# Cluster masks of an attention kernel computed in strips of 32 rows instead of 64, for two units at once

## The chip, the cores and the metric

The kernel runs on one core of one Trainium2 chip. The metric is the device time of one execution in microseconds (us). Times inside the execution come from one profiled run, whose span from the first to the last instruction was 786.4 us; TensorE was granted 0.997 of its full clock.

## The reference

The program is an attention block in which a query sees only the keys of its own cluster, followed by a router over eight experts. Cut to what matters here:

```python
# q, k, v: (B=4, H=8, S=768, D=64); centroids: (8, 16, 64)
q_assign = argmax(q_n @ c_n.T)          # cluster of each query, 16 clusters a head
k_assign = argmax(k_n @ c_n.T)          # cluster of each key
mask = q_assign[..., :, None] == k_assign[..., None, :]
scores = 0.125 * q @ k.T
attn = softmax(where(mask, scores, -1e9))
x = (attn @ v)                          # then (B,H,S,D) -> (3072, 512)
# router: each row of x goes to one of 8 experts:
# out[rows of e] = gate * relu(x[rows] @ w1[e]) @ w2[e]
```

## The kernel before

**Two stages.** Attention takes roughly the first 360 us and the experts the rest; only attention is touched. The 32 pairs of batch and head are taken two heads at a time, which gives 16 head pairs. Each head pair has 2 halves of 384 queries and 6 blocks of 128 keys, 12 units, 192 in all. A unit is the scores of 128 keys by 384 queries for both heads. Its accumulator `s_ps` is 2 banks of PSUM (the accumulator memory that TensorE writes), one for each head, and the pool has two such buffers, so two units fill all four banks.

**The mask as a product.** The mask isn't applied by a selection. Every token has a code of three numbers (the columns 0, 1, 2 of `cd`), made so that the product of the codes of a key and a query is minus a huge number times the squared difference of the two cluster numbers: zero in the same cluster and hugely negative in any other. That product is added in the accumulator to the scores, and exp makes of it zero. `cd` holds a token's code in 64 columns for each of two heads, of which three are used; turned so that codes stand on partitions, head 0 takes rows 0 to 63 and head 1 rows 64 to 127. `choose` (L342, L345) writes the code columns from the cluster numbers `pm` on ScalarE, a transposing DMA turns them into `hot`, and `keys` (L375) copies the keys' half into `kH` on GpSimd. For the first head pair TensorE turns them (L362).

**A unit on TensorE.** `scores` (L437) issues for one unit four products: the two masks (`s_ps<-hot,kH`, bf16) and the two scores (`s_ps<-qT,kT`, f32), all with 64 rows of contraction. The two heads use the two halves of the rows of the array, so that they run side by side. `expo` (L448) is ScalarE's exp of the finished unit into `prob` (five buffers). `attend` (L457) multiplies `prob` with the values: 128 rows of contraction, 64 columns a head, both heads side by side in the columns. VectorE adds the `prob` tiles up in `acc` (L466, L476) for the denominators, and `total` (L491) sums those over partitions on TensorE in four column strips of 32.

**The order of the work** is written out by hand for all five engines. The main loop takes two units an iteration, 96 iterations. An iteration issues, in this order: for each of the two units two places ahead, `scores` and then `expo`; a piece of other work (`between`: cluster products L319 of the next head pair, codes, routing of an earlier batch); and `attend` of the two current units. At every third iteration `total` follows. So TensorE runs in one iteration: masks and scores of unit m, masks and scores of unit m+1, then the values' products of units m-2 and m-1. Unit m's masks write the buffer that unit m-2's exp has read, and unit m+1's masks that of unit m-1. The last iteration has no scores left to issue, so there are 95 such groups; units 0 and 1 come in `begin`.

Of the kernel before, what the change touches and what calls it, by code (L numbers as in the profile page):

```python
# [9 lines left out]
F32 = mybir.dt.float32  # L10
BF16 = mybir.dt.bfloat16
# [7 lines left out]
P = 128  # L19

SQ = 32
# [18 lines left out]
def kernel(  # L40
# [121 lines left out]
    tau = smp.tile([E, 1], F32, name="tau", bufs=1)  # L162


    cd = const.tile([P, S // (2 * SQ), 2, D], BF16, name="cd")
    wcd = const.tile([P, 1], F32, name="wcd")
    cn_r = smp.tile([P, 1], F32, name="cn_r", bufs=1)
    cn2 = smp.tile([P, 2, D], F32, name="cn2", bufs=1)
# [22 lines left out]
    def constants():  # L191
        nc.vector.memset(onesb, 1.0)
        keep_up(9)
        nc.vector.memset(epsc, EPS)
        make_identity(nc, ident)
        nc.gpsimd.iota(io_i, pattern=[[1, P]], base=0, channel_multiplier=0)

        nc.gpsimd.iota(
            tok_i.rearrange("p (b j) -> p b j", j=NJ),
            pattern=[[S, B], [P, NJ]],  # L200
            base=0,
            channel_multiplier=1,
        )
        for i, (p0, w) in enumerate(((0, -BIG), (D, -2.0))):
            nc.gpsimd.memset(wcd[p0 : p0 + D], w)
        make_identity(nc, identb)
        nc.gpsimd.memset(cd, 0.0)
        for i, (p0, c) in enumerate(((0, -BIG), (D, -1.0))):
            nc.gpsimd.memset(cd[p0 : p0 + D, :, :, 2 - 2 * i : 3 - 2 * i], c)
        make_upper_triangular(nc, sltb, val=1.0, diag=False)  # L210
        nc.gpsimd.memset(tri, 0.0)
        for e in range(1, E):
            nc.gpsimd.memset(tri[:, e, 0:e], 1.0)
        nc.vector.memset(cnB, 0.0)
        nc.vector.memset(ones, 1.0)
        nc.vector.memset(embT, 0.0)
        nc.vector.memset(cumx[:, 0], 0.0)
        nc.vector.memset(eb[:, 0:2], 0.0)
        nc.vector.tensor_copy(io_b, io_i)
        nc.vector.tensor_copy(io_f, io_i[0:1, 0:NBLK])  # L220
        nc.vector.tensor_scalar(prefc, io_b[:, 0:C], -1.0, float(C), ALU.mult, ALU.add)
        nc.vector.tensor_scalar(prefe, io_b[:, 0:E], -1.0, float(E), ALU.mult, ALU.add)
# [34 lines left out]
    def begin():  # L257

        nc.scalar.dma_start(out=c_sb, in_=centroids.rearrange("h c d -> (h c) d"))
        load(0, "q")  # L260
        load(0, "k")
        load(0, "v")
        load(1, "qk")
        constants()

        nc.scalar.activation(en_r, epsc[0:E], ACTF.Sqrt)
        nc.scalar.dma_start(out=emb, in_=moe_expert_emb)
        nc.scalar.dma_start(out=tau, in_=moe_tau.to_broadcast([E, 1]))
        norm_rows(cn_r, c_sb, P)
        unit_centroids()  # L270
        keep_up(2)
        piece(0, "turn0")
        piece(0, "turn1")
        norm_rows(en_r, emb, E)

        nc.scalar.activation(cn_r, epsc, ACTF.Exp)
        piece(0, "products")
        for m in range(2):
            scores(m, (1,))
        piece(0, "choose")  # L280
        keep_up(6)
        piece(0, "turn_numbers")
        for m in range(2):
            scores(m, (0,))
            expo(m)
        piece(0, "values")
        token_numbers()
        unit_experts()

    def prep_pieces(n):  # L290
# [39 lines left out]
        def choose():  # L330

            shp = [P, S // SQ, C]
            asn = t["asn"].rearrange("p (g c) -> p g c", c=C)
            amax = smp.tile(shp[0:2], F32, tag="amax", name="amax")
            sel = smp.tile(shp, BF16, tag="sel", name="sel", bufs=1)
            pm = smp.tile(shp[0:2], BF16, tag="pm", name="pm")
            nc.vector.tensor_reduce(amax, asn, axis=AXX, op=ALU.max)
            nc.vector.tensor_tensor(sel, asn, bc(amax, shp, 2), ALU.is_equal)
            nc.vector.tensor_tensor(sel, sel, bc(prefc, shp, 1), ALU.mult)
            nc.vector.tensor_reduce(pm, sel, axis=AXX, op=ALU.max)  # L340
            pm = pm.rearrange("p (s h) -> p s h", h=2)
            nc.scalar.activation(cd[..., 1], pm, ACTF.Copy, scale=wcd)  # L342
            for i, p0 in enumerate((0, D)):
                g = slice(p0, p0 + D)
                nc.scalar.activation(  # L345
                    cd[g, :, :, 2 * i], pm[g], ACTF.Square, scale=(BIG**0.5, 1.0)[i]
                )
            t["H"] = trp.tile([P, S // (2 * SQ), P], BF16, tag="hot", name="hot")
            if n > 0:
                nc.sync.dma_start_transpose(  # L350
                    out=t["H"], in_=cd.rearrange("p s h c -> p (s h c)")
                )

        def turn_numbers():

            t["kH"] = trp.tile([P, S], BF16, tag="kH", name="kH")
            kH = t["kH"].rearrange("r (i s t) -> r s i t", i=2, t=SQ)
            U = S // (4 * SQ)
            for half in range(2):
                bk = misc().bitcast(BF16)  # L360
                for u in range(U):
                    nc.tensor.transpose(  # L362
                        bk[:, P * u : P * u + P],
                        cd[:, U * half + u].rearrange("p h c -> p (h c)"),
                        identb,
                    )
                bk = bk[:, 0 : P * U].rearrange("r (s x) -> r s x", x=P)
                ss = slice(U * half, U * half + U)
                nc.scalar.copy(kH[:, ss], bk[:, :, D:].rearrange("r s (i t) -> r s i t", t=SQ))
                nc.vector.tensor_copy(t["H"][:, ss, 0:D], bk[:, :, 0:D])  # L370
# [49 lines left out]
    gr = [dict() for _ in range(ngroups)]  # L420
    xT = {}

    def scores(i, parts=(0, 1)):

        n, hq, j = units[i]
        t = ld[n]
        if "s_ps" not in un[i]:
            un[i]["s_ps"] = psS.tile([P, 2, 512], F32, tag="s_ps", name="s_ps")
        s_ps = un[i]["s_ps"]
        for part in parts:  # L430
            if part == 0:
                l, r = t["kH"], t["H"][:, :, SQ * hq : SQ * hq + SQ]
            else:
                l, r = t["kT"], t["qT"][:, HS * hq : HS * hq + HS]
            for h in range(2):
                rows = slice(D * h, D * h + D)
                nc.tensor.matmul(  # L437
                    s_ps[:, h, 0:HS],
                    lhsT=l[rows, P * j : P * j + P],
                    rhs=r[rows],  # L440
                    start=part == (1 if len(parts) < 2 else 0),
                    stop=part == (0 if len(parts) < 2 else 1),
                )

    def expo(i):
        d = un[i]
# [482 lines left out]
    def piece(n, name, *args):  # L929
        if n < NP:  # L930
            if n not in prepare:
                prepare[n] = prep_pieces(n)
            prepare[n][name](*args)
# [67 lines left out]
    with tc.manual_schedule(engines=by_hand):  # L1001
        begin()
        for i in range(0, len(units), 2):
            n, it = divmod(i // 2, NJ)
            if it == 0 and n + 2 < NP:
                load(n + 2, "qk")
            if it == 1 and n + 1 < NP:
                load(n + 1, "v")
            if it == 3 and n in (1, 2, 3, 5, 6, 7, 9, 10):

                slot, part = divmod(n - 1 - n // 4, 4)
                w, c, x = ((w1s, KD, moe_w1), (w2s, KF, moe_w2))[part // 2]
                cs = slice(c // 2 * (part % 2), c // 2 * (part % 2) + c // 2)
                nc.scalar.dma_start(
                    out=w[slot][:, cs], in_=x[0].rearrange("(c p) f -> p c f", p=P)[:, cs]
                )
            for m in range(i + 2, min(i + 4, len(units))):
                scores(m)
                expo(m)
            between(n, it)  # L1020
            if i > GU and i % GU == (2 if i // GU + 2 >= ngroups else 4):
                divide(i // GU - 1)
            b, nb = divmod(n, NHP)
            if (b, nb, it) in early:
                early[b, nb, it]()
            if i + 2 == len(units):
                ats.close()
                tile_waits = {"side": "right", "reuse_waits": "tile"}
                psX = ctx.enter_context(tc.tile_pool(name="psX", bufs=1, space=PSUM, **tile_waits))
                turn_x(0, nc.scalar.copy, xp.tile([P, DM], F32, tag="acc", name="xTm"))  # L1030
            for m in range(i, i + 2):
                attend(m)
            if i + 2 == len(units):
                rows(ngroups - 2)
                route[b][0](0)
            if i % GU == 0 and i > 0:
                total(i // GU - 1)
# [125 lines left out]
```

The softmax here doesn't subtract the row's maximum and nothing guards it: scores larger than these inputs give would overflow.

## Time and profile before

| What | Value |
|---|---|
| Three runs before | 787.69, 787.95, 789.35 us; median 787.95 |
| Profiled run | 788.4 us; span 786.4 us |
| `s_ps<-qT,kT` (scores, f32, 64 rows, 384 columns), L437 | 768 records, mean 482 ns |
| `s_ps<-hot,kH` (masks, bf16, 64 rows, 384 columns), L437 | 384 records, mean 328 ns |
| `o_ps<-prob,v` (values, f32), L457 | 768 records, mean 499 ns |
| exp of a unit, ScalarE, L448 | 192, mean 810 ns |
| sum of a unit into `acc`, VectorE, L476 | 128, mean 1012 ns |

How to read it: the profile counts an engine busy from the start of an instruction to its end, and for TensorE the ends are modelled. Two matmuls that run side by side are two records that start a few nanoseconds apart. What a matmul costs in a dense stretch is the distance between starts, not its duration. An f32 product appears as two records. PE is TensorE's matmul side and PEld its loading of weights, DVE is VectorE, ACT is ScalarE, POOL is GpSimd; L437 is line 437 of the kernel.

### The profile page before, as it was taken

The page shows a single profiled execution, that of the slowest core. Times are in us where ns is not written, and L with a number is a line of the kernel's source. Part 1 is how long each engine was busy: PE and PEld are TensorE (multiplying, and loading weights), DVE is VectorE, ACT ScalarE, POOL GpSimd, SP SyncE. Part 2 cuts the span into 40 slices and gives each one's busy share as a digit, 9 for nine tenths or more (in the row PEclk, how much of TensorE's full clock was granted, in tenths as well). Part 3 has the DMA queues.
Part 4 walks back from the last instruction along what each step waited for, and adds up shares of the span by engine and source line. Part 5 has one row for each costly group of instructions (what it writes and reads, how often), then busy time and mean ns, then how long its engine had stood idle before and what let it go on. Part 6 is the DMA issues. An engine that isn't in the chain of part 4 may idle for free.

```text
span 786.4 us, 12732 instructions
## 1 busy us (share of the span) xinstructions
PE 768.4 (98%) x4850; PEld 442.3 (56%) x4850; DVE 349.8 (44%) x614; ACT 259.7 (33%) x417; POOL 183.1 (23%) x402
## 2 busy tenths in 40 slices
PE   7999999999999999999999999999999999999995
PEld 3444444443444334436776776776776776776772
DVE  5688889998889998878430000000000000000000
ACT  5445455564457455563151111111110111111110
POOL 3233323434344233440111211211211211211200
PEclk9999999999999999999999999999999999999998
DMA  9466878877869456485797965988656763146400
GB/s 154 74 131 139 145 110 151 156 148 150 128 140 202 74 92 118 105 248 121 267 332 273 372 226 206 320 320 312 212 220 241 259 244 133 51 143 237 149 15 24
DMA packets 241888, 140.42 MB, mean 179 GB/s; under 512 B 202389, under 2 KB 203925, under 8 KB 241824
## 3 DMA queue, kind: packets, MB, share of 16 engines
q1 hardware_dynamic: 233968, 117.27, 58.5%
q0 software_dynamic: 4480, 13.87, 4.9%
q10 hardware_dynamic: 3376, 8.44, 3.1%
q8 instruction: 40, 0.66, 0.4%
q14 instruction: 24, 0.20, 0.1%
HBM read 158.61 MB, written 13.83 MB: 219 GB/s over the span
## 4 chain that ended last, share of the span: by engine, by line
PE 41%; issue 28%; DMA 23%; DVE 5%; POOL 1%; ACT 0%; SPq 0%; POOLq 0%; DVEq 0%; ACTq 0%
PE s_ps L437 17%; DMA out_dram<-y,sidx 17%; PE o_ps L457 14%; PE h_ps L871 3%; DMA out_dram<-y,gidx 2%; DVE acc L476 2%; PE y_ps L887 2%; PE misc L491 2%; PE misc L319 1%; DMA x_rows<-gate 1%; DMA w1s<-in_moe_w_dram 1%; PE misc L566 1%; DMA w2s<-in_moe_w_dram 1%; DMA q<-in_q_dram 1%; DMA k<-in_k_dram 1%
## 5 line engine op out<-in xcount | busy, mean ns | idle before, releaser
L871 PEld LDWEIGHTS h_ps<-xTm,w1s 128*128 128x128 f32 x1792 | 202.6, 192 | 20.8 <-DVE xTm L859 18.0
L871 PE MATMUL h_ps<-xTm,w1s 128*128 128x128 f32 x1792 | 208.0, 277 | 0.0
L887 PE MATMUL y_ps<-w2s,hT 128*128 128x512 f32 x448 | 201.1, 593 | 0.0
L448 ACT ACTIVATE prob<-s_ps 128x768 f32<-128x768 f32 x192 | 153.8, 810 | 143.1 <-PE s_ps L437 122.4
L859 DVE COPY xTm<-x_ps 128x512 f32<-128x512 f32 x24 | 16.6, 691 | 330.9 <-PE x_ps L857 330.9
L437 PE MATMUL s_ps<-qT,kT 64*128 64x384 f32 x768 | 155.1, 483 | 0.0
L457 PE MATMUL o_ps<-prob,v 128*64 128x384 f32 x768 | 145.1, 499 | 0.8 <-DVE xT L530 0.8
L476 DVE TENSOR_TENSOR acc<-acc,prob 128x768 f32<-128x768 f32 x128 | 129.6, 1012 | 6.4
L887 PEld LDWEIGHTS y_ps<-w2s,hT 128*128 128x128 f32 x448 | 81.0, 190 | 81.8 <-issue 81.8
L878 ACT ACTIVATE hT<-h_ps 128x512 f32<-128x512 f32 x56 | 33.4, 597 | 204.0 <-PE h_ps L871 204.0
L457 PEld LDWEIGHTS o_ps<-prob,v 128*64 128x64 f32 x768 | 46.5, 136 | 84.5 <-issue 69.4
L898 POOL DMA_INDIRECT out_dram<-y,sidx x24 | 23.8, 990 | 290.3 <-ACT y L897 284.4
L514 POOL COPY inv<-inv 32x6 f32<-32x6 f32 x232 | 56.2, 242 | 114.2 <-DVE inv L511 103.5
L437 PEld LDWEIGHTS s_ps<-qT,kT 64*128 64x128 f32 x768 | 68.8, 189 | 20.9 <-issue 20.6
L897 ACT ACTIVATE y<-y_ps,xin 128x512 f32<-128x512 f32 x28 | 19.2, 686 | 146.4 <-PE y_ps L887 140.1
L437 PE MATMUL s_ps<-hot,kH 64*128 64x384 bf16 x384 | 63.5, 328 | 2.3 <-ACT prob L448 1.3
L437 PEld LDWEIGHTS <-kH 64*128 64x128 bf16 x384 | 19.4, 93 | 64.0 <-issue 45.2
L375 POOL COPY kH<-hot 128x768 bf16<-128x768 bf16 x15 | 14.2, 947 | 95.5 <-DMA hot<-cd 83.0
L821 POOL DMA_INDIRECT xin<-x_rows,gidx x28 | 29.8, 1063 | 25.9 <-DMA x_rows<-gate 9.1
L466 DVE SCALAR_TENSOR_TENSOR acc<-prob 128x768 f32<-128x768 f32 x32 | 30.3, 947 | 0.0
L857 PEld LDWEIGHTS x_ps<-ident,xin 128*128 128x128 f32 x112 | 13.9, 141 | 13.8 <-issue 13.2
L491 PE MATMUL misc<-acc,ones 128*32 128x192 f32 (+1 forms) x244 | 18.0, 346 | 2.5 <-DVE acc L476 2.4
(192 smaller groups left out, 413.7 us busy)
## 6 DMA issues: line engine op xcount, KB each, us to landing
w1s<-in_moe_w_dram SPq DMA_DIRECT2D x28, 2048.0 KB
w2s<-in_moe_w_dram SPq DMA_DIRECT2D x28, 2048.0 KB
v<-in_v_dram SPq DMA_DIRECT2D x32, 192.0 KB
x_rows<-xb SPq DMA_DIRECT2D x128, 48.0 KB
q<-in_q_dram SPq DMA_DIRECT2D x60, 96.0 KB
k<-in_k_dram SPq DMA_DIRECT2D x60, 96.0 KB
xr<-x_rows SPq DMA_DIRECT2D x9, 512.0 KB
w1s<-in_moe_w_dram ACTq DMA_DIRECT2D x4, 1024.0 KB
```

What stands on the lines that cost most here:

```text
L437: nc.tensor.matmul(s_ps[:, h, 0:HS], lhsT=l[rows, P * j : P * j + P], rhs=r[rows], start=part == (1 if len(parts) < 2 else 0), stop=part = ...
L448: nc.scalar.activation(d["prob"], d["s_ps"][:, :, 0:HS], ACTF.Exp, scale=scale)
L457: nc.tensor.matmul(g["o_ps"][D * h : D * h + D, 0:HS], lhsT=ld[n]["v"][:, j, h], rhs=d["prob"][:, h], start=(j == 0), stop=(j == NJ - 1),)
L466: nc.vector.scalar_tensor_tensor(out=g["acc"], in0=un[i - 1]["prob"], scalar=NJ * EPS, in1=d["prob"], op0=ALU.add, op1=ALU.add,)
L476: nc.vector.tensor_tensor(g["acc"], g["acc"], d["prob"], ALU.add)
L491: nc.tensor.matmul(bk[M * i : M * i + M, 0:W], lhsT=ones[:, 0:M], rhs=d["acc"][:, i * W // HS, c : c + W], start=True, stop=True,)
L514: nc.gpsimd.tensor_copy(inv2[M * to : M * to + M, W // SQ * (i % 2) : W // SQ * (i % 2 + 1)], inv[M * i : M * i + M],)
L821: nc.gpsimd.indirect_dma_start(out=xin, out_offset=None, in_=x_rows[0:n], in_offset=bass.IndirectOffsetOnAxis(ap=gidxs[part][:, c : c + 1] ...
L871: nc.tensor.matmul(bk[:, m : m + P], lhsT=w1s[j % 2][:, c, f0 + m : f0 + m + P], rhs=d["xT"][:, P * c : P * c + P], start=(c == 0), stop=( ...
L878: nc.scalar.activation(d["hT"][:, f0 : f0 + 512], bk, ACTF.Relu)
L887: nc.tensor.matmul(bk, lhsT=d["hT"][:, P * c : P * c + P], rhs=w2s[j % 2][:, c], start=(c == 0), stop=(c == KF - 1),)
L898: nc.gpsimd.indirect_dma_start(out=out[:], out_offset=bass.IndirectOffsetOnAxis(ap=to, axis=0), in_=y, in_offset=None, bounds_check=N - 1, ...
```

## The change

A token's code now has 32 columns a head instead of 64, and `cd` holds it twice: its 128 columns are two copies of (head 0, head 1), 32 columns each. Turned, rows 0 to 31 are head 0, rows 32 to 63 head 1, and rows 64 to 127 the same again. The masks of a unit with an even number use the first copy and those of an odd one the second. `scores` takes both units of an iteration and issues first their four masks, each with 32 rows of contraction in a strip of its own, and then the four scores, which are as before. The two `expo` follow after both units' products. `choose` writes every code column twice, by reading `pm` with a repeat. In `begin`, the scores of units 0 and 1 are issued as before, and their masks together.

```diff
-    cd = const.tile([P, S // (2 * SQ), 2, D], BF16, name="cd")
+    cd = const.tile([P, S // (2 * SQ), 2, 2, SQ], BF16, name="cd")
...
-            nc.gpsimd.memset(cd[p0 : p0 + D, :, :, 2 - 2 * i : 3 - 2 * i], c)
+            nc.gpsimd.memset(cd[p0 : p0 + D, :, :, :, 2 - 2 * i : 3 - 2 * i], c)
...
-        for m in range(2):
-            scores(m, (1,))
+        scores((0, 1), (1,))
         piece(0, "choose")
         keep_up(6)
         piece(0, "turn_numbers")
+        scores((0, 1), (0,))
         for m in range(2):
-            scores(m, (0,))
             expo(m)
...
-            pm = pm.rearrange("p (s h) -> p s h", h=2)
+            pm = bc(pm.rearrange("p (s h) -> p s h", h=2), [P, S // (2 * SQ), 2, 2], 2)
             nc.scalar.activation(cd[..., 1], pm, ACTF.Copy, scale=wcd)
...
-    def scores(i, parts=(0, 1)):
+    def scores(us, parts=(0, 1)):
...
         for part in parts:
-            if part == 0:
-                l, r = t["kH"], t["H"][:, :, SQ * hq : SQ * hq + SQ]
-            else:
-                l, r = t["kT"], t["qT"][:, HS * hq : HS * hq + HS]
-            for h in range(2):
-                rows = slice(D * h, D * h + D)
+            for i in us:
+                n, hq, j = units[i]
+                t = ld[n]
+                if part == 0:
+                    l, r = t["kH"], t["H"][:, :, SQ * hq : SQ * hq + SQ]
+                else:
+                    l, r = t["kT"], t["qT"][:, HS * hq : HS * hq + HS]
+                for h in range(2):
+                    rows = slice(D * h, D * h + D)
+                    if part == 0:
+                        rows = slice(D * (i % 2) + SQ * h, D * (i % 2) + SQ * h + SQ)
+                    nc.tensor.matmul(
...
-            for m in range(i + 2, min(i + 4, len(units))):
-                scores(m)
+            us = range(i + 2, min(i + 4, len(units)))
+            scores(us)
+            for m in us:
                 expo(m)
```

More of the change, by code (lines that the diff above doesn't have):

```diff
@@ L345, in choose @@
                 nc.scalar.activation(
-                    cd[g, :, :, 2 * i], pm[g], ACTF.Square, scale=(BIG**0.5, 1.0)[i]
+                    cd[g, :, :, :, 2 * i], pm[g], ACTF.Square, scale=(BIG**0.5, 1.0)[i]
                 )
@@ L350, in choose @@
                 nc.sync.dma_start_transpose(
-                    out=t["H"], in_=cd.rearrange("p s h c -> p (s h c)")
+                    out=t["H"], in_=cd.rearrange("p s r h c -> p (s r h c)")
                 )
@@ L363, in turn_numbers @@
                         bk[:, P * u : P * u + P],
-                        cd[:, U * half + u].rearrange("p h c -> p (h c)"),
+                        cd[:, U * half + u].rearrange("p r h c -> p (r h c)"),
                         identb,
@@ L421 @@
     xT = {}
-    def scores(i, parts=(0, 1)):
[L425 to L429, printed above, removed]
-        for part in parts:
-            if part == 0:
-                l, r = t["kH"], t["H"][:, :, SQ * hq : SQ * hq + SQ]
-            else:
-                l, r = t["kT"], t["qT"][:, HS * hq : HS * hq + HS]
-            for h in range(2):
-                rows = slice(D * h, D * h + D)
[L437 to L443, printed above, removed]
+    def scores(us, parts=(0, 1)):
+        for i in us:
+            if "s_ps" not in un[i]:
+                un[i]["s_ps"] = psS.tile([P, 2, 512], F32, tag="s_ps", name="s_ps")
+        for part in parts:
+            for i in us:
+                n, hq, j = units[i]
[9 more added lines that the diff above has]
+                    nc.tensor.matmul(
+                        un[i]["s_ps"][:, h, 0:HS],
+                        lhsT=l[rows, P * j : P * j + P],
+                        rhs=r[rows],
+                        start=part == (1 if len(parts) < 2 else 0),
+                        stop=part == (0 if len(parts) < 2 else 1),
+                    )
     def expo(i):
```

## The prediction

> **What bounds the kernel now.** I read the page's busy shares first, then the stretch of attention that the change touches.
>
> ```profile
> PE 768.4 (98%) x4850; PEld 442.3 (56%) x4850; DVE 349.8 (44%) x614; ACT 259.7 (33%) x417; POOL 183.1 (23%) x402
> ...
> PE   7999999999999999999999999999999999999995
> ...
> DVE  5688889998889998878430000000000000000000
> ```
>
> ```profile
> 50.00:340.00 290.00, 287.16 (x2018) 117.36 (x2014) 258.75 (x441) 159.13 (x250) 109.09 (x283) 1.00 0.73 134
> ```
>
> The second fence is the busy time of PE, PEld, DVE, ACT and POOL from 50 to 340 us, then TensorE's clock. TensorE is busy for 287.16 of 290 us at full clock and VectorE for 258.75 (89%). TensorE sets the pace and VectorE isn't far behind. After attention TensorE stays full (397.5 of 400 us from 380 to 780 us), so a delay in attention isn't won back later.
>
> A busy TensorE still has gaps that records hide. They show in the timeline of one plain iteration (start, time, operation, tiles, shapes, count):
>
> ```profile
> 153.09 0.34 PE L437 MATMUL s_ps<-hot,kH 64*128 64x384 bf16 x2
> 153.27 0.81 PE L437 MATMUL s_ps<-qT,kT 64*128 64x384 f32 x4
> 153.91 0.33 PE L437 MATMUL s_ps<-hot,kH 64*128 64x384 bf16 x2
> 154.07 0.81 PE L437 MATMUL s_ps<-qT,kT 64*128 64x384 f32 x4
> 154.81 1.51 PE L457 MATMUL o_ps<-prob,v 128*64 128x384 f32 x8
> 156.26 0.34 PE L437 MATMUL s_ps<-hot,kH 64*128 64x384 bf16 x2
> ```
>
> An iteration takes 3.17 us. Inside the scores group all products have the shape of 64 rows by 128 columns, and each starts 0.16 us before the modelled end of the one ahead (masks end at 153.43, scores start at 153.27). A pair of masks therefore costs 0.16 to 0.18 us, a pair of scores 0.64. Where the shape changes, the next starts only 0.07 us before that end: the scores end at 154.88 and the values start at 154.81; the values end at 156.32 and the masks start at 156.26. **Every change of shape costs 0.09 us of draining**, and there are two an iteration. A second cost sits in the first record after it, since its weights weren't loaded ahead. For just these scores products it shows in `begin`, where they follow products of another shape (128 rows, 32 columns). The first two fences below are timelines, the third the statistics of L437 there (minimum, median, maximum in ns):
>
> ```profile
> 9.35 0.49 PE L319 MATMUL misc<-kT,cnB 128*32 128x384 f32 x1
> ```
>
> ```profile
> 9.76 0.59 PE L437 MATMUL s_ps<-qT,kT 64*128 64x384 f32 x2
> ```
>
> ```profile
> L437 PE MATMUL s_ps<-qT,kT x8: 482/482/587, 9.8 to 10.8; 64*128 64x384 f32 x8
> ```
>
> They start 0.08 us before the end at 9.84, and the first record takes 587 ns instead of 482: 0.105 us more.
>
> **What the Trainium skill says.** "TensorEngine Tiling (Array Packing)", section Key Properties: changing the tiling mode, not just the tile, drains TensorE. The trace agrees, with the 0.09 us above. "TensorE: Matmul & The Clock Gate", Part 3, Measured speedup: four row strips of 32 ran 3.07 times as fast as one after the other, each starting some 4 ns after the last. No run here shows four row strips; two row strips (L437) and four column strips (L319) do run side by side. The same page, Part 2, LDWEIGHTS: a load takes as long for 32 rows as for 128, since the columns count; the 64-row mask loads took 93 ns here, and I keep that for 32 rows.
>
> **The change part by part.**
>
> *Removed:* one of two mask slots, since four masks stand side by side: 0.16 us in each of 95 groups, 15.4 us.
>
> *Added:* a third change of shape, from 32-row strips to 64-row halves, between masks and scores. The trace has one change between these widths, at the expert embedding's turns (8 rows in use[...]):
>
> ```profile
> 25.16 0.81 PE L437 MATMUL s_ps<-qT,kT 64*128 64x384 f32 x4
> 25.90 0.41 PE L250 MATMUL misc<-ident,emb 8*128 8x8 f32 x4
> 26.25 0.87 PE L457 MATMUL o_ps<-prob,v 128*64 128x384 f32 x4
> ```
>
> The scores end at 25.97 and the turn starts at 25.90: 0.07 before, so it drains as well. The bounds of the new switch are nothing and 0.09 + 0.105 = 0.195 us; I take the upper one, as every change of shape in the trace drains.
>
> *New group:* the four masks start over some 15 ns (an estimate: four side by side at L319 start over 0.02 us); the last ends 0.33 later; scores start 0.07 before that, at 0.28. Then 0.105 for the first weights, 0.64 for the first unit, and 0.74 for the second with the switch to the values (154.07 to 154.81): 1.765 us. Before it was 154.81 - 153.09 = 1.72. The difference is **+0.045 us a group, +4.3 us over 95**.
>
> *A new wait.* The second unit's masks now stand ahead of the first unit's scores, and they wait for the exp of the unit before. Behind them on TensorE's queue stand both units' scores, the pieces of `between` and the values; both exps wait for the scores. In a plain iteration that exp ended 0.51 us before the group begins. The later scores push the exps by 0.18 us, which leaves some 0.35, so nothing. It costs where ACT is late, first at the start:
>
> ```profile
> 15.90 1.51 ACT L448 ACTIVATE prob<-s_ps 128x768 f32<-128x768 f32 x2 [0.82 <-PE s_ps L437]
> 16.76 0.34 PE L437 MATMUL s_ps<-hot,kH 64*128 64x384 bf16 x2 [0.74 <-ACT prob L448]
> ```
>
> TensorE starts here 0.05 us after the first exp (16.71). It will wait for the second (17.41) and reach the values at 17.46 + 1.765 = 19.22 instead of 18.48: 0.74, of which 0.045 is counted, so 0.7 us. Comparing the starts of groups with the ends of exps in the timeline, the second exp still ran in nine more groups (at 145.1, 166.2, 177.3, 237.1, 254.0, 274.1, 321.7, 343.3, 355.1), by 0.18 to 0.78 us, and at 265.9 the group itself waits inside. Each overhang plus 0.05 sums to some 5.4 us. That is the upper bound; the lower is nothing, because most are exps held up by `acc` (ACT waits there 16.7 us in all for DVE), and DVE gains 0.045 us an iteration; also the iterations at 254.0, 265.9 and 343.3 last 5.60, 5.00 and 5.43 us instead of 4.72, so TensorE waits there later anyway. I take 1.5 us.
>
> *Codes.* Three ACT writes a head pair grow from 24 to 48 elements. At exp's rate (768 in 810 ns) that is 25 ns each, an estimate. For head pairs 1 to 15 it is hidden by the wait of POOL for `hot` and the exps' slack. For head pair 0 TensorE waits for them (1.0 us at L362): 0.1 us. The transposing DMA moves as much as before, the copies of L375 also, and the memsets of `cd` come long before `choose`. `begin`'s masks save 0.16 us that only the second exp could see, and it queues behind the first.
>
> *Sum:* 4.3 + 0.7 + 1.5 + 0.1 = 6.6 us; 786.4 becomes 793.0. The three runs' median lies 1.55 above the span, so 787.95 + 6.6 = **794.5 us**. Its own range: the group by 0.03 to 0.06 us (2.9 to 5.7), the later waits by 0 to 5.4, so 791 to 800.
>
> **The rivals.**
>
> *Free switch, faster.* If strips of 32 and 64 rows count as one shape, as both span all 128 columns and differ in rows alone, then neither drain nor late weights come: -0.16 + 0.015 a group, -14.0 us. The waits give back 2.3, so 776. VectorE at 89% would then stand at 93%, so that 778 is as likely. Against it speak the turn at 25.90 and that every such change drains. It decides as soon as the switch costs under 0.12 us: 0.145 less the waits' 2.3/95.
>
> *Half a switch.* Only the drain (0.09) or only the late weights (0.105): -5.1 or -4.1, with the waits 785 or 786.
>
> *No four strips.* If the masks run in pairs only, the change doesn't do what it says and 0.16 us a group is added to the forecast: +15.4, 810. Against it speaks the skill's measurement and the four strips at L319; for it, that no row strips of 32 side by side are in the trace.
>
> **How the numbers follow.** Forecast 0.74, free switch 0.10, half a switch 0.08, pairs only 0.08. The range runs from 784.5, below the half switch, to 802, above the forecast's own range, and leaves out the free switch and the pairs. About 0.2% (1.6 us) is what a measurement can tell from no change. Faster is the free switch and most of the half one, 0.16; the same is the rest of it and a forecast with a cheap switch, 0.07; slower 0.77.
>
> **What would show it.** In the profile after: four masks that start within 0.02 us (else pairs); scores that start 0.28 after them, not 0.17, with a first record near 587 ns (else a free or half switch); a plain iteration of 3.21 us instead of 3.17; a wait of PE for `prob` near 17.4 us and a few later ones. The forecast is wrong if the iteration gets shorter, or if the waits at L437 reach several us more than taken.

## The result

The changed kernel is slower: 797.42 us (median of 4 runs, 797.15 to 797.80) against 788.19 us (4 runs, 787.69 to 789.35) on the same chip, a ratio of 1.0115 with a 95% interval of 1.0098 to 1.0133. Run again beside other experiments on another chip it took 797.34 us against 788.86, 1.0101 (1.0084 to 1.0119). The span of the profiled run is 795.3 us, 8.9 more than before. The forecast was 794.5 us: the right side and inside its range, 2.9 us too low.

**The profile after.** First the page's busy shares, with TensorE's clock in 40 slices of the span:

```profile
PE 777.7 (98%) x4850; PEld 440.7 (55%) x4850; DVE 349.6 (44%) x614; ACT 257.8 (32%) x417; POOL 182.7 (23%) x402
...
PEclk8999999999999999999999999999999999999998
```

The shares have hardly moved and TensorE still bounds the kernel. New is the 8 at the head of the clock's row, where the kernel before had a 9. A plain iteration in the timeline (start, time, operation, tiles, shapes, count) shows the rest; the line numbers move by a few lines from kernel to kernel:

```profile
155.01 0.34 PE L440 MATMUL s_ps<-hot,kH 32*128 32x384 bf16 x4
155.28 1.56 PE L440 MATMUL s_ps<-qT,kT 64*128 64x384 f32 x8
156.77 1.51 PE L460 MATMUL o_ps<-prob,v 128*64 128x384 f32 x8
158.21 0.34 PE L440 MATMUL s_ps<-hot,kH 32*128 32x384 bf16 x4
```

The four masks do stand side by side: four records that start within 0.01 us of each other take 0.34 us, where two took 0.34 before. But the scores start 0.27 us after the masks, not 0.16 to 0.18, and 0.07 us before the masks' modelled end (155.35), so the switch of strip width drains. The statistics of L440 from 50 to 340 us (minimum, median, maximum in ns) show the late weights as well:

```profile
L440 PE MATMUL s_ps<-qT,kT x632: 482/482/587, 49.5 to 338.5; 64*128 64x384 f32 x158
```

The first record after the switch takes 587 ns instead of 482. Its weights come late: they start to load when the scores do, while in the kernel before the load of the first scores' weights began at 153.10, 0.17 us ahead of the scores at 153.27:

```profile
153.10 0.36 PEld L437 LDWEIGHTS s_ps<-qT,kT 64*128 64x128 f32 x4
```

```profile
155.28 0.95 PEld L440 LDWEIGHTS s_ps<-qT,kT 64*128 64x128 f32 x8 [0.17 <-issue]
```

From masks to values the group lasts 156.77 - 155.01 = 1.76 us, where it was 1.72; the iteration 3.20 us where it was 3.17 (3.162 and 3.206 as the medians of 53 plain iterations, with the trace's nanoseconds).

**Where the 8.9 us came in.** Setting the starts of the same groups side by side in the two timelines:

| Start of | Before | After | Later by |
|---|---|---|---|
| scores of units 0 and 1 | 9.76 | 9.97 | 0.2 |
| masks of units 0 and 1 | 15.52 | 16.03 | 0.5 |
| values of the first iteration | 18.48 | 21.43 | 2.9 |
| masks of the second iteration | 19.93 | 23.37 | 3.4 |
| the last group of masks | 358.92 | 367.78 | 8.9 |
| end of the span | 786.4 | 795.3 | 8.9 |

Over a third of the loss is in by 23.4 us, before the second iteration has begun. The rest, 5.4 us, builds up over 94 groups at a net 0.043 us each (4.0) and from waits (the remaining 1.4). After attention nothing is lost or won back.

Most of the start's loss is the clock's. The busy times of PE, PEld, DVE, ACT and POOL, with TensorE's granted clock as the third number from the right, in two stretches of 5 us, before the change and after:

```profile
15.00:20.00 5.00, 3.74 (x26) 1.69 (x27) 4.44 (x13) 3.21 (x5) 0.00 (x0) 1.00 1.50 153
20.00:25.00 5.00, 5.00 (x36) 2.15 (x38) 2.33 (x4) 1.62 (x2) 0.00 (x0) 1.00 0.12 21
```

```profile
15.00:20.00 5.00, 2.90 (x13) 1.25 (x14) 4.57 (x13) 2.10 (x4) 0.00 (x0) 0.57 1.25 155
20.00:25.00 5.00, 5.00 (x26) 1.80 (x22) 0.14 (x1) 2.01 (x3) 0.00 (x0) 0.75 0.10 18
```

The clock was at half for 6.83 us, from 15.66 to 22.49.

The waits of TensorE, before the change and after (who waits for whom, us in all, times, longest), in the two answers on waits:

```profile
PE misc L491 <- DVE acc L476: 2.4, 4, 0.8
PE s_ps L437 <- ACT prob L448: 1.3, 3, 0.7
```

```profile
PE s_ps L440 <- ACT prob L451: 3.0, 7, 0.9
...
PE misc L494 <- DVE acc L479: 0.8, 2, 0.4
```

The wait for exp grew by 1.7 us, 0.35 of it at the start, and the one for VectorE's `acc` shrank by 1.6. What the new wait costs is partly a wait that would have come later anyway. Set side by side iteration by iteration, nine later groups (at 145.1, 166.2, 232.4, 254.0, 265.9, 274.1, 321.7, 343.3 and 355.1 us of the kernel before) are longer by 0.09 to 0.72 us beyond the 0.043, 3.6 us in all. Of these, 2.2 us come back in the same iterations or later ones, where the kernel before waited and the changed one waits less. One place, where the exp is late behind a load of ScalarE's tables:

```profile
169.38 1.28 ACT L451 ACT_TABLE_LOAD   x1
...
170.67 1.51 ACT L451 ACTIVATE prob<-s_ps 128x768 f32<-128x768 f32 x2
171.53 0.34 PE L440 MATMUL s_ps<-hot,kH 32*128 32x384 bf16 x2
172.23 0.34 PE L440 MATMUL s_ps<-hot,kH 32*128 32x384 bf16 x2 [0.36 <-ACT prob L451]
172.50 1.56 PE L440 MATMUL s_ps<-qT,kT 64*128 64x384 f32 x8
```

The first unit's masks start as soon as the first of the two exps ends (171.48). The second unit's wait until 172.23 for the other (172.18), and behind them all eight records of scores, the first unit's too, for which everything was ready.

### The profile page after: what moved, and what is told of

Read it like the earlier page. It is cut to its first block, busy times and chain, and to the rows that moved or that the text cites. A ratio compares the mean times of both kernels' runs of the same rounds, so it can differ in the third digit from the quotient of the medians.

```text
span 795.3 us, 12732 instructions
## 1 busy us (share of the span) xinstructions
PE 777.7 (98%) x4850; PEld 440.7 (55%) x4850; DVE 349.6 (44%) x614; ACT 257.8 (32%) x417; POOL 182.7 (23%) x402
## 4 chain that ended last, share of the span: by engine, by line
PE 41%; issue 28%; DMA 22%; DVE 5%; ACT 1%; POOL 1%; POOLq 0%; SPq 0%; DVEq 0%; ACTq 0%
PE s_ps L440 17%; DMA out_dram<-y,sidx 17%; PE o_ps L460 13%; PE h_ps L874 3%; PE misc L494 2%; DVE acc L479 2%; DMA out_dram<-y,gidx 2%; PE y_ps L890 2%; PE misc L318 2%; DMA x_rows<-gate 1%; DMA w2s<-in_moe_w_dram 1%; PE misc L569 1%; ACT prob L451 1%; PE misc L390 1%; DMA k<-in_k_dram 1%
## 5 line engine op out<-in xcount | busy, mean ns | idle before, releaser
L451 ACT ACTIVATE prob<-s_ps 128x768 f32<-128x768 f32 x192 | 147.1, 808 | 158.2 <-PE s_ps L440 121.1
L440 PE MATMUL s_ps<-qT,kT 64*128 64x384 f32 x768 | 151.2, 512 | 0.0
L440 PEld LDWEIGHTS s_ps<-qT,kT 64*128 64x128 f32 x768 | 66.6, 187 | 42.3 <-issue 17.8
L440 PEld LDWEIGHTS <-kH 32*128 32x128 bf16 x384 | 10.8, 91 | 54.5 <-issue 48.4
L440 PE MATMUL s_ps<-hot,kH 32*128 32x384 bf16 x384 | 36.1, 334 | 4.1 <-ACT prob L451 3.0
L860 PEld LDWEIGHTS x_ps<-ident,xin 128*128 128x128 f32 x112 | 13.9, 141 | 13.8 <-issue 13.2
L312 DVE STREAM_TRANSPOSE qT<-q 128x768 f32<-128x768 f32 x15 | 14.7, 977 | 13.1 <-PE s_ps L440 11.9
```

The source lines that it names most:

```text
L440: nc.tensor.matmul(un[i]["s_ps"][:, h, 0:HS], lhsT=l[rows, P * j : P * j + P], rhs=r[rows], start=part == (1 if len(parts) < 2 else 0), st ...
L451: nc.scalar.activation(d["prob"], d["s_ps"][:, :, 0:HS], ACTF.Exp, scale=scale)
```

## The experiments

Two theories stood at the start. The first: the switch of width costs 0.043 us a group net, the new wait some 2 us, and the half clock at the start some 2.2. The rival: the new order and its wait are the main cost, and the switch is cheap.

### The order alone

The kernel before with the order of the changed one: the masks of both units first, but 64 rows wide.

```diff
-    cd = const.tile([P, S // (2 * SQ), 2, 2, SQ], BF16, name="cd")
+    cd = const.tile([P, S // (2 * SQ), 2, D], BF16, name="cd")
...
                     rows = slice(D * h, D * h + D)
-                    if part == 0:
-                        rows = slice(D * (i % 2) + SQ * h, D * (i % 2) + SQ * h + SQ)
```

> The order of the changed kernel (four masks, then both units' scores) with the codes and the 64-row masks of the kernel before; nothing is left out. Theory (the change of strip width costs each group 0.043 us net, the wait for the second exp some 2 us in all, and the half clock at the start some 2.2 us): no change of width is left, so a plain iteration is back at 3.163 us; the waits stay, 0.7 us at the start and some 1.4 later, so about 790.3 us, or 792.5 if the clock drops at the start here too. Rival (the order and its waits are the main cost): 795 to 797, the waits stay and the iteration makes up little.

Measured: 791.42 us (6 runs, 789.58 to 793.05), 1.0029 (1.0013 to 1.0046). Its timeline:

```profile
152.92 0.50 PE L438 MATMUL s_ps<-hot,kH 64*128 64x384 bf16 x4
153.25 1.45 PE L438 MATMUL s_ps<-qT,kT 64*128 64x384 f32 x8
154.63 1.51 PE L458 MATMUL o_ps<-prob,v 128*64 128x384 f32 x8
156.08 0.50 PE L438 MATMUL s_ps<-hot,kH 64*128 64x384 bf16 x4
```

The masks take two slots (0.33 us to the scores), there is no switch, and the iteration is back at 3.16 us. TensorE waits for `prob` 3.4 us in 8 places, more than in the changed kernel. From the second iteration to the last group the profiled run loses 1.8 us to the kernel before, all of it waits, since the iteration is as long. So the wait is real and costs about what was expected, and the rival falls: the order alone makes 2.4 us of 9, in medians. In the profiled run the clock was halved here as well, from 15.5 us on, although up to the first masks (15.54 us) the program is that of the kernel before. So that start can lose its clock too, and part of the 2.4 us may be that: the six executions ran at mean clocks from 0.993 (793.05 us) to 0.997 (789.58).

### The switch three times

The changed kernel's strips, taken unit by unit.

```diff
-            scores(us)
             for m in us:
+                scores((m,))
                 expo(m)
```

> The codes and 32-row strips of the changed kernel, but unit by unit as before: masks of one unit, its scores, masks of the other, its scores. Nothing is left out. Each group has three more changes of shape than before instead of one: into the scores twice (0.09 drain + 0.105 late weights each) and back to the masks once (0.09 + 0.01). Theory: +0.50 us a group, a plain iteration of 3.66 us, +47 us over 95 groups, less some 3 us of waits that vanish as ScalarE and VectorE get slack: 831 to 838 us. Rival (the switch is cheap and the waits are the cost): the wait for the second exp is gone here, so at most a few us over before, 788 to 795.

Measured: 835.15 us (2 runs), 1.0588 (1.0563 to 1.0612), 46 us over the kernel before. The timeline:

```profile
163.05 0.34 PE L440 MATMUL s_ps<-hot,kH 32*128 32x384 bf16 x2
163.32 0.92 PE L440 MATMUL s_ps<-qT,kT 64*128 64x384 f32 x4
164.16 0.34 PE L440 MATMUL s_ps<-hot,kH 32*128 32x384 bf16 x2
164.43 0.92 PE L440 MATMUL s_ps<-qT,kT 64*128 64x384 f32 x4
165.28 1.51 PE L460 MATMUL o_ps<-prob,v 128*64 128x384 f32 x8
166.72 0.34 PE L440 MATMUL s_ps<-hot,kH 32*128 32x384 bf16 x2
```

Read it as the first timeline of the kernel before: masks to scores 0.27 us both times instead of 0.17, scores to the next thing 0.84 or 0.85 instead of 0.64 or 0.74, and the iteration 3.67 us, 0.50 more. Two switches into the scores at 0.195 us and one back to the masks at 0.10 make 0.49 us, and 0.50 was measured: the prices hold in a second order of the same products. The profiled run had its clock halved at the start as well.

### Where the clock was lost

Five runs asked whether the half clock comes from TensorE's idle time in `begin`. The kernel issues filler products there (`keep_up`); the first adds four to the six ahead of the turned codes.

```diff
-        keep_up(6)
+        keep_up(10)
         piece(0, "turn_numbers")
```

> The changed kernel with ten filler products at the start of TensorE's queue after the cluster products of the first head pair, instead of six; they fit into its wait for the codes. Theory (TensorE's clock was halved from 15.7 to 22.5 us because it idled longer there): the clock stays full, 2.2 us come back, 795.2 us, granted clock 0.997. Rival (the drop comes from the wait for the second exp, which comes later): the clock drops all the same, 797.4.

Measured: 796.53 us (4 runs, 794.97 to 798.43), 1.0106 (1.0084 to 1.0128). The profiled run, the fastest at 794.97, kept its clock; the spread doesn't tell whether the others did. Not conclusive.

The next gave the kernel before the longer code writes alone, each code twice in a head's own 64 columns:

```diff
-            pm = pm.rearrange("p (s h) -> p s h", h=2)
+            pm = bc(pm.rearrange("p (s h) -> p s h", h=2), [P, S // (2 * SQ), 2, 2], 3)
```

> The kernel before, with every code column written twice (each head's 64 columns hold the three numbers at 0 to 2 and at 32 to 34), so that ScalarE writes 48 elements a row as in the changed kernel; the masks' products double, which changes no result of exp. Theory: the writes hide in head pairs 1 to 15 and cost 0.3 us ahead of the first masks: 788.5 us if the clock holds, some 790.5 if the longer idling alone halves it. Rival (the longer writes delay exps in every head pair): 16 pairs by 0.3 us, 793.

Measured: 791.12 us (8 runs, 789.18 to 792.70), 1.0022 (1.0007 to 1.0036). The profiled run (792.70) had its clock halved from 15.9 us on; the next masks came at 23.07 us, 3.1 later than before, and from there to the last group it lost only 0.8 us more. So nothing like 0.3 us a head pair is paid. The drop came here with the longer writes and the old order, and in the run of the order alone with the old writes and the new order, so neither of the two is needed for it. The mean clocks of the eight executions, 0.991 to 0.997, suggest that it doesn't come in each.

Last, the changed kernel again, and both kernels with filler in both idle stretches (the edit is the same in both):

```diff
-        keep_up(6)
+        keep_up(10)
         piece(0, "turn_numbers")
+        keep_up(4)
```

> The changed kernel itself once more, beside the kernel before and the two runs below on one chip, so that the part of the half clock at the start can be told from chance. If the drop at the start comes in every execution of it, some 797.4 us with little spread; if only in some, 795 to 798 in two groups some 2.2 us apart.

> The changed kernel with filler on TensorE in both of its waits at the start: ten products instead of six ahead of the turned codes, and four more between those and the first masks. Theory (the clock is halved because of these two idle stretches): no drop at the start in any execution, 795.0 us, 2.2 less than the changed kernel where that drops. Rival (the drop isn't the start's idle time, or costs nothing): the same as the changed kernel.

> The kernel before with the same filler. If its own spread (787.7 to 791.1) is the same drop of the clock in some executions, its upper values go and the median falls by 0 to 1.3 us, to 787.5 to 788.5 us; if the spread has another cause, no change.

Measured on one chip, with the mean granted clock of the runs:

| Kernel | Median us (runs) | Lowest to highest | Clock |
|---|---|---|---|
| changed, again | 797.34 (5) | 797.29 to 798.01 | 0.993 in all |
| changed, filler twice | 795.10 (6) | 794.74 to 796.49 | 0.995 to 0.998 |
| before | 788.86 (27) | 787.37 to 791.77 | 0.992 to 0.998 |
| before, filler twice | 788.27 (22) | 787.64 to 789.00 | 0.996 to 0.998 |

The windows of the changed kernel with filler twice:

```profile
15.00:20.00 5.00, 3.60 (x24) 1.43 (x24) 4.69 (x13) 2.90 (x6) 0.00 (x0) 1.00 1.49 151
20.00:25.00 5.00, 5.00 (x38) 2.00 (x34) 1.29 (x4) 2.10 (x3) 0.00 (x0) 1.00 0.15 24
```

The clock stays at 1.00 in the profiled run, and 797.34 - 795.10 = 2.2 us come back. With the clock kept, the new wait can be measured by itself:

```profile
15.90 0.35 PE L441 MATMUL s_ps<-hot,kH 32*128 32x384 bf16 x4
...
21.05 0.34 PE L441 MATMUL s_ps<-hot,kH 32*128 32x384 bf16 x4
```

From the masks of units 0 and 1 to those of the second iteration it takes 5.14 us (with the trace's nanoseconds), and 4.40 in the kernel before (15.52 to 19.93): 0.74 us more. In the changed kernel, at half clock, it took 7.35.

The changed kernel has a mean clock of 0.993, that of its profiled run with the drop, in each of its five executions. In the kernel before the times spread over 4.4 us with a clock of 0.992 to 0.998, and with the filler the times above 789.0 are gone. That kernel beats both: 0.9988 (0.9981 to 0.9996) of the kernel before, little but clear of noise. That its longer executions lost their clock at the start is likely, but not shown: its profiled run didn't.

One start loses its clock, and another with the same idle stretches doesn't. The ten traces show a part of the reason. In all six profiled runs with a drop it came 10.24 us after the clock had become full (in the changed kernel from 5.42 to 15.66) and lasted 6.83 us, three times and two times 3.41 us, as if the clock were decided every 3.41 us. In the last 3.41 us before the drop TensorE was idle for 1.90 to 2.24 us. In the four runs without a drop no such stretch of the start, counted from the moment of full clock, has more than 1.74 us. The busy times of the two stretches in the kernel before, of the last one in the order alone, and of the last one in the changed kernel (the first number is the length, the second PE's busy time):

```profile
10.83:14.24 3.41, 2.44 (x20) 1.09 (x17) 1.68 (x4) 0.84 (x4) 0.12 (x1) 1.00 1.58 141
14.24:17.65 3.41, 1.67 (x18) 1.03 (x16) 2.72 (x11) 2.35 (x4) 0.00 (x0) 1.00 1.55 140
```

```profile
12.10:15.51 3.41, 1.47 (x15) 0.88 (x14) 1.27 (x4) 1.68 (x5) 0.00 (x0) 1.00 1.56 143
```

```profile
12.25:15.66 3.41, 1.51 (x16) 0.87 (x14) 0.95 (x3) 1.98 (x5) 0.00 (x0) 1.00 1.23 144
```

The kernel before and the order alone have the same idle stretches of 0.96 and 1.00 us here. But the clock became full at 4.00 us in the one and at 5.27 in the other, so that the stretches fell into two counts in the one (0.97 and 1.74 us idle) and into one count in the other (1.94). By this reading it is chance which of the two happens, since the moment of full clock differs from run to run (4.00 to 6.69 us), and the longer writes make a loss likelier, as the first stretch grows from 0.96 to 1.26 us. No run tested it, and no exact limit follows: at the end of the span of the changed kernel with filler, 1.92 us (782.5 to 785.9) passed without a drop.

### Scores in the same strips

If the switch eats the gain, a group without it should gain. This run keeps 32-row strips through the scores; it leaves half of each head's 64 numbers out of them and counts the other half twice.

```diff
-                    if part == 0:
+                    if part == 0 or n > 0:
                         rows = slice(D * (i % 2) + SQ * h, D * (i % 2) + SQ * h + SQ)
...
-            scores(us)
+            scores(us, (0, 1) if n_of(us) == 0 else (0, 1, 2))
```

> The changed kernel, but from the second head pair on the scores run in the four 32-row strips of the masks too: each head of each unit uses one strip of keys and queries twice, instead of its own 64 rows, so half of the head's 64 numbers are left out of the scores and others counted double; the amount of work in TensorE time is the same (two products of 384 columns for each of four strips), and the shape doesn't change between masks and scores. Theory (the switch eats the gain of the four strips): the iteration falls to 3.163 - 0.162 + 0.015 = 3.02 us, 0.19 less than in the changed kernel, 13 us less than before over 90 groups; 1 to 3 us at the start and 1.5 to 6 us of waits for exps and VectorE, which is at 94% then, are given back: 777 to 785 us. Rival (four strips can't stream f32 scores side by side, or their weight loads collide): an iteration of 3.2 us or more, no faster than the changed kernel.

Measured: 796.60 us (4 runs, 796.16 to 799.82), 1.0102 (1.0073 to 1.0132). Neither expectation held. The timeline of TensorE and ScalarE:

```profile
197.66 0.34 PE L443 MATMUL s_ps<-hot,kH 32*128 32x384 bf16 x4
197.83 1.46 PE L443 MATMUL s_ps<-qT,kT 32*128 32x384 f32 x16
199.22 1.51 PE L463 MATMUL o_ps<-prob,v 128*64 128x384 f32 x8
199.34 1.51 ACT L454 ACTIVATE prob<-s_ps 128x768 f32<-128x768 f32 x2 [3.10 <-PE s_ps L443]
200.67 0.57 PE L443 MATMUL s_ps<-hot,kH 32*128 32x384 bf16 x4
...
202.51 1.51 ACT L454 ACTIVATE prob<-s_ps 128x768 f32<-128x768 f32 x2 [0.49 <-PE s_ps L443]
203.90 0.51 PE L443 MATMUL s_ps<-hot,kH 32*128 32x384 bf16 x4
```

TensorE's part was right: scores 0.17 us after the masks, masks to values 1.56 us, and the iteration from 197.66 to 200.67 takes 3.01 us. But all four strips finish together, so both exps start only when the whole group is done (199.34) and end at 200.85, after the next group has begun. Its second masks wait, and that iteration takes 3.23 us. Of the 53 plain iterations 27 take 3.00 us and 18 take 3.17 to 3.40: the wait that cost 1.4 us in the changed kernel comes in these 18, and in most of the iterations with other products. From the second iteration to the last group the profiled run loses 1.5 us to the kernel before, where the changed kernel loses 5.4. Without the switch the four strips do save on TensorE, 0.157 us an iteration or some 14 us over 90 (an estimate from the plain iterations of 3.162 and 3.005 us), and waits took all of it. The run also lost its clock at the start (next masks at 23.91), and TensorE waited 2.1 us for the first gathered rows of the experts. A version that hands over one unit earlier, or spreads the other products of TensorE over the iterations, wasn't tried.

## Why the prediction was right, and what it missed

- **Bound.** TensorE sets the pace: right. It was busy for 288.23 us from 50 to 340 us, and what it lost in attention stayed lost.
- **Four strips side by side.** Right: four masks take the slot of two, so one slot of 0.16 us is gone. Pairs only, the rival of 810 us, is out.
- **The switch.** Right, and in both its parts: 0.07 us before the modelled end and a first record of 587 ns, as forecast from two other places of the trace. That the first weights aren't loaded ahead is in the trace of the weight loads. One of the two places was the 8-row turn; no run shows that its rows count as a strip of 32, but the runs now show the switch itself. The free and half switch are out; their sums in the forecast are off by up to 0.3 us (95 times -0.145 is -13.8, not -14.0), which changes nothing. The group was forecast at 1.765 us and took 1.76; +4.3 was forecast over 95 groups, 4.0 was found over 94.
- **The wait for the second exp.** Right in kind. The 1.5 us for the later ones was chosen between 0 and 5.4, not summed, so that it came so near to the 1.4 found is partly luck; the order alone loses 1.8 in its trace. Of the ten groups that the forecast named, eight grew longer; those at 177.3 and 237.1 didn't, and one that it hadn't named, at 232.4, did. The forecast misread one line: 4.72 us is the plain length for the products of the iteration at 254.0, while one with the products of that at 265.9 takes 3.62, so the wait there was longer than it took it to be. In the changed kernel the waits for `prob` grew while those for `acc` shrank, as the forecast had argued for taking less than the full 5.4.
- **The start.** Mis-sized: 0.7 for the wait and 0.1 for the codes, 3.2 us found (without the 0.2 by which already the first scores started later). The wait itself was right: 0.74 us with the clock kept, 0.045 of it the group's, as forecast. The codes took 0.3, as the three writes overlap: 0.10 us more at the first write and 0.14 at each of the other two, not 0.025, so exp's rate for long rows was the wrong price for these short writes. The other 2.2 us is a term that the sum didn't have. The forecast priced the longer wait ahead of the turned codes only as a wait, and took TensorE's clock as given.

The sum with the clock kept was right to half a microsecond: 6.6 us forecast, and 795.10 us with the filler against 788.27 us of the kernel before with the same filler is 6.8.

## What to carry to other kernels

Count changes of shape on TensorE, not just products: packing masks into four strips saved 0.16 us and put in a switch of 0.195. With the scores in the same strips the iteration was 0.16 us shorter than before, until the exps' wait came. When products of several units are issued ahead together, the first unit inherits the wait of the last, and if they finish together their exps start late together. This kernel's start, with its filler, sits close to the point where the clock drops: 0.3 us more of ScalarE's writes there came with 2.2 us of clock. Work added to such a stretch has to be priced with the clock.

## What the runs showed of the hardware

- A switch between 32-row and 64-row strips of the same 128 columns costs what a switch between row and column strips did: the next product starts 0.07 us before the modelled end instead of 0.16, and the first f32 record of 128 columns takes 587 ns instead of 482. The weights of that record start to load with it instead of 0.17 us ahead. For bf16 masks of 128 columns it was 332 ns instead of 323.
- Four 32-row strips stream f32 products of 384 columns side by side: 16 records in 1.46 us.
- TensorE's clock was halved for 6.83 us though no idle stretch of TensorE ahead of the drop was longer than 1.3 us (1.26 us and the first 0.64 of the next one in the changed kernel). It came in all five profiled runs with the longer code writes and no added filler, in one without longer writes (the order alone), and in none of the three with added filler, and cost 2.2 us. Six drops came 10.24 us after full clock, with 1.90 to 2.24 us of the last 3.41 us idle.
- ScalarE's code writes of 48 elements a row instead of 24 took 0.10 to 0.14 us longer, where exp of 768 elements takes 810 ns.
